# Six of seven expert searches on packed free tokens, low bits of each threshold from eight candidates, and eleven staging places for the gates' weights

## The chip, the core and the metric

The kernel runs on one core of a Trainium2 chip. The metric is device time in microseconds (us) of one execution. The engines are named as in the profile: PE (TensorE), DVE (VectorE), ACT (ScalarE), POOL (GpSimd) and SP (SyncE, which here issues DMAs). PEld is the weight load of TensorE.

## The reference

Three layers follow one another over 20224 tokens (4 sequences of 5056) of width 256. The first is a gated recurrence along each sequence. The other two are mixtures of 8 experts, each a two-layer network 256 to 1024 to 256.

```python
for t in range(S):                       # 1: recurrence
    h = f[:, t] * h + i[:, t] * x[:, t]
cap = N // E                             # 2: greedy assignment, 2528 tokens per expert
for idx in np.argsort(-logits.flatten()):
    tok, e = idx // E, idx % E
    if assigned[tok] >= 0 or counts[e] >= cap:
        continue
    assigned[tok] = e; counts[e] += 1
out[assigned == e] = np.maximum(x[mask] @ w1[e], 0) @ w2[e]
gate_w = softmax(x @ w_gate).max(-1)     # 3: best expert of each token, weighted
out[expert_idx == e] = gate_w * (np.maximum(x[mask] @ w1[e], 0) @ w2[e])
```

The greedy assignment is what the change is about. It falls into eight phases: in each, every free token wants its best expert among those not full; the next expert to fill has a threshold logit, all wishes above it are granted, and that expert leaves. Phases 0 to 6 need a search for the threshold; phase 7 gives the rest to the last expert.

## The kernel before, in words

**Stages.** A first stage reads the inputs in 40 pieces and runs the recurrence (`block`, lines 259 to 333). Then the first mixture (`moe1`) runs 16 lists: lists 0 to 7 hold, for each expert, 1024 tokens that a quick partial search already knows (`quick`, table `idxa`); lists 8 to 15 hold, in the order in which the experts fill, the other tokens (`compact_b`, table `idxb`). A list is made of blocks of 256 tokens: 4 blocks in each of lists 0 to 7, 6 in each of lists 8 to 15, 80 in all. A block fetches its rows by two indirect DMAs on POOL (L1218), turns them on PE (L1165), multiplies by the first weights (`up`, L1188) and the second (`down`, L1206), each product split in three float32r matmuls (high, low, cross), so a block has 48 matmuls of L1188 and 48 of L1206. `hand` scatters the result by four indirect DMAs per two blocks (L1298). The second mixture (`slot2`) runs 83 more blocks.

**What sets the order.** PE, DVE, ACT and POOL run in an order written out beforehand: `Plan.add` takes each operation with an assumed cost, its dependences and a priority, and `emit` fixes one order for each engine. A small number is a high priority: `up`'s outputs have -1, block work 1 or 2, splits of weights and the gates 3, a search 5 (`BG`), and compaction 6 (`CB`). An indirect DMA is planned at 1.05 us of POOL. On the chip each engine keeps that order and waits where an operand is late. SP issues its DMAs in order as well.

**The search, `assign(ph)`.** The best logits of the free tokens stand in a table of 1280 columns (`lay8`, phases 0 to 3) or 640 (`lay4`, phases 4 to 6, after `relay`). Eight rounds fix the high 16 bits of the threshold, two bits a round: `count` compares the table with three values, one on DVE (L710) and two on ACT (L715), `sums` adds on PE (L721, L724), and DVE decides (L743). Eight more rounds fix the low 16 bits in the same way (L783). `update` removes what was granted, over all 160 columns and 8 experts. In phase 0 the first six rounds have the highest priority, and `quick` follows them.

**The gates.** `gates` multiplies all second weights of the first mixture by the gate weights of the second, in two halves of eight chunks. Each chunk (512 KB, L1025) is loaded to one of four staging places (two halves of `rb`, two of `sh`), transposed on PE (L1032, 8 of them), copied by ACT (L1036, 2) and multiplied (L1037, 4). The first `down` of the first block needs the first half, its later ones the second half.

**Weights.** `load_w(e)` reads the weights of expert e (L1059, L1060) into `r1` and `r2`, splits them into high and low parts (L1063 on ACT; L1065 on POOL for expert 0, L1067 on DVE) and stores the parts for later (L1083); `load_again` reads them back for lists 8 to 15 (L1105), after SP has read the expert's number `ei` (L1091).

## Time and profile before

| | us |
|---|---|
| median of three runs | 2357.04 (2356.72 to 2360.22) |
| the profiled execution | 2358.22 |
| its span, first to last instruction | 2356.4 |
| PE busy in the span | 2190.8 (93%) |
| DVE busy | 1412.1 (60%) |
| ACT busy | 1022.0 (43%) |
| POOL busy | 601.2 (26%) |

The page gives each engine's busy time and its share in 40 slices. A window of the trace gives the busy time of each engine in one stretch and the number of its instructions; with one source line it counts that line's instructions alone, so blocks can be counted: 48 matmuls of L1188 are one block. The waits name the engine and the line that ended an idle time. Matmuls are pipelined, so PE can be shown as busy while its instructions start further apart than at best.

### The profile page before, as it was taken

How to read it: one execution, taken by the hardware profiler on the slowest of the kernel's cores; microseconds unless marked ns; L12 is line 12 of the kernel's file. 1: busy time of each engine (PE TensorE's matmuls, PEld its weight loads, DVE VectorE, ACT ScalarE, POOL GpSimd, SP SyncE). 2: the span in 40 equal slices, each digit the busy share in tenths (PEclk: the TensorE clock that was granted, in tenths of full speed). 3: DMA queues.
4: the chain of work that ended last, by engine and by line, in shares of the span. 5: the costliest groups of instructions: out<-in, count | busy, mean ns of one | idle time of the engine just before them, and what ended most of it. 6: DMA issues, size and time to landing. Idle time of an engine off the chain costs nothing.

```text
span 2356.4 us, 48919 instructions
## 1 busy us (share of the span) xinstructions
PE 2190.8 (93%) x18005; PEld 2115.6 (90%) x18005; DVE 1412.1 (60%) x3985; ACT 1022.0 (43%) x2094; POOL 601.2 (26%) x721
## 2 busy tenths in 40 slices
PE   7886899999999999995868899999999999999998
PEld 6774579999999999995758899999999999999998
DVE  7898778787887786876664444344433443344432
ACT  4555656746746635464532222223322232223322
POOL 5333313333432332141214112111111111111111
PEclk9998999999999999997879999999999999999999
DMA  9889635544567543544223318411425232311240
GB/s 323 268 272 329 226 135 179 206 158 145 203 222 233 193 170 123 198 146 158 74 101 125 106 33 287 120 46 46 119 53 173 57 114 53 118 47 46 49 122 26
DMA packets 262713, 341.84 MB, mean 145 GB/s; under 512 B 128220, under 2 KB 220254, under 8 KB 250688
## 3 DMA queue, kind: packets, MB, share of 16 engines
q1 hardware_dynamic: 235824, 264.10, 35.4%
q0 software_dynamic: 26640, 74.52, 9.2%
q8 instruction: 144, 2.36, 0.4%
q14 instruction: 105, 0.86, 0.1%
HBM read 495.90 MB, written 133.35 MB: 267 GB/s over the span
## 4 chain that ended last, share of the span: by engine, by line
PE 37%; issue 35%; DVE 9%; POOL 5%; DMA 4%; ACT 2%; SPq 1%; POOLq 0%; DVEq 0%; ACTq 0%
PE yp L1206 17%; PE bank L1188 16%; POOL out_dram L1541 5%; PE bank L1165 1%; DVE hl L1193 1%; DMA rb<-in_moe_w_dram 1%; DMA xg<-x1d,idxb 1%; DMA xg<-xs 1%; DMA w2l<-wsp 1%; PE bank L1037 1%; ACT ohb L715 1%; DVE jkc L997 1%; DMA xs<-xr,di 0%; PE bank L1032 0%; PE pb L308 0%
## 5 line engine op out<-in xcount | busy, mean ns | idle before, releaser
L1193 DVE SCALAR_TENSOR_TENSOR hl<-bank,hh 128x512 fp32r<-128x512 f32 x652 | 449.5, 689 | 729.8 <-ACT hh L1192 728.8
L1192 ACT ACTIVATE hh<-bank 128x512 fp32r<-128x512 f32 x652 | 389.0, 597 | 870.1 <-PE bank L1188 863.3
L1206 PE MATMUL yp<-w2h,hh 128*128 128x264 f32 (+1 forms) x2176 | 622.4, 286 | 6.9 <-ACT xr L1256 3.0
L1188 PE MATMUL bank<-xh,w1h 128*128 128x256 f32 x2176 | 616.9, 284 | 9.6 <-DVE hl L1193 9.6
L1188 PE MATMUL bank<-xl,w1h 128*128 128x256 f32 x2176 | 619.7, 285 | 0.9 <-DVE xl L1175 0.9
L1206 PE MATMUL yp<-w2l,hh 128*128 128x264 f32 (+1 forms) x2176 | 619.7, 285 | 0.0
L1206 PE MATMUL yp<-w2h,hl 128*128 128x264 f32 (+1 forms) x2176 | 618.9, 284 | 0.0
L1188 PE MATMUL bank<-xh,w1l 128*128 128x256 f32 x2176 | 615.0, 283 | 0.0
L1188 PEld LDWEIGHTS bank<-xh,w1h 128*128 128x128 f32 x2176 | 413.5, 190 | 9.8 <-DVE hl L1193 9.8
L1206 PEld LDWEIGHTS yp<-w2h,hh 128*128 128x128 f32 x2176 | 412.2, 189 | 8.5 <-ACT xr L1256 3.2
L1188 PEld LDWEIGHTS bank<-xl,w1h 128*128 128x128 f32 x2176 | 414.1, 190 | 1.3 <-DVE xl L1175 1.3
L1188 PEld LDWEIGHTS bank<-xh,w1l 128*128 128x128 f32 x2176 | 414.5, 190 | 0.0
L1206 PEld LDWEIGHTS yp<-w2l,hh 128*128 128x128 f32 x2176 | 412.0, 189 | 0.0
L1206 PEld LDWEIGHTS yp<-w2h,hl 128*128 128x128 f32 x2176 | 411.0, 189 | 0.0
L1541 POOL DMA_INDIRECT out_dram<-xr,ii x166 | 163.5, 985 | 761.3 <-ACT xr L1535 714.6
L1298 POOL DMA_INDIRECT xs<-xr,di x160 | 168.0, 1050 | 403.0 <-issue 173.3
L1188 PE MATMUL bank<-xh,third 128*128 128x256 f32 x864 | 168.2, 280 | 2.5 <-ACT xh L1174 2.5
L1206 PE MATMUL yp<-third,hh 128*128 128x256 f32 x864 | 156.6, 279 | 0.0
L1218 POOL DMA_INDIRECT xg<-x1d,idxb x96 | 96.2, 1002 | 231.1 <-PE bank L1165 140.1
L1188 PEld LDWEIGHTS bank<-xh,third 128*128 128x128 f32 x864 | 140.2, 190 | 2.7 <-ACT xh L1174 2.7
L715 ACT ACTIVATE ohb<-U,lw 128x1280 f16<-128x1280 uint16 (+1 forms) x104 | 115.6, 1112 | 44.0 <-DVE lw L786 37.5
L1206 PEld LDWEIGHTS yp<-third,hh 128*128 128x128 f32 x864 | 132.1, 189 | 0.0
(399 smaller groups left out, 3059.1 us busy)
## 6 DMA issues: line engine op xcount, KB each, us to landing
third<-wsp SPq DMA_DIRECT2D x108, 1024.0 KB
w1h<-wsp SPq DMA_DIRECT2D x53, 1024.0 KB
w1l<-wsp SPq DMA_DIRECT2D x53, 1024.0 KB
w2h<-wsp SPq DMA_DIRECT2D x53, 1024.0 KB
w2l<-wsp SPq DMA_DIRECT2D x53, 1024.0 KB
xg<-xs SPq DMA_DIRECT2D x332, 64.0 KB
fl<-in_f_logit_dram SPq DMA_DIRECT2D x36, 512.0 KB
xl<-in_x_dram SPq DMA_DIRECT2D x36, 512.0 KB
```

What stands on the lines that cost most here:

```text
L715: lambda k=k: act.activation(jk2[:, :TN], src[:, :TN], AF.Sign, bias=t3[:, k:k + 1], scale=sc, accum_out=ca3[:, k:k + 1]),
L997: dve(0.3, lambda a=a, a0=a0, px=px: v.scalar_tensor_tensor(jk[a % 2], px()[:, a, 0:J], q1[:, a0 + a:a0 + a + 1], arow, op0=OP.is_equal, o ...
L1037: P.add("PE", GC[1], lambda e=e, h=h, gt=gt, acc=acc: pe.matmul(acc.tile[:E * E], wgz[:, h, (7 - e) * E:(15 - e) * E], gt, start=e == 0 an ...
L1165: pe.transpose(bk.tile[:, o:o + 128], x2[i4][:, k, h * 128:(h + 1) * 128], identf)
L1188: P.add("PE", 0.1192, lambda c=c, h=h, k=k, w_=w_, xx=xx, s_=s_: pe.matmul(bk.tile[:, c * G:(c + 1) * G], wt(q, w_)[:, h, s_], xx[i4][:, h ...
L1192: P.add("ACT", 0.48, lambda: act.activation(hh[hb], bk.tile, AF.Relu), [bk], [("hh", hb)], prio=-1)
L1193: P.add("DVE", 0.6, lambda: v.scalar_tensor_tensor(hl[hb], bk.tile, 0.0, hh[hb].bitcast(F32), op0=OP.max, op1=OP.subtract), [bk, ("hh", hb ...
L1206: P.add("PE", 0.1192 if wid == D else 0.1215, lambda i=i, s_=s_, k=k, x_=x_, w_=w_, fc=fc: pe.matmul(yp[:ms[i], i, 0:wid], x_[hb][:, s_], ...
L1218: P.add("POOL", 1.05, lambda i=i, j=j: pool.indirect_dma_start(out=x2[i4][:, i, :D], out_offset=None, in_=x1d, in_offset=bass.IndirectOffs ...
L1298: st = pool.indirect_dma_start(out=xs, out_offset=bass.IndirectOffsetOnAxis(ap=di[i2][:, i:i + 1], axis=0), in_=y[:, i, 0:D + 2], in_offse ...
L1541: st = pool.indirect_dma_start(out=out, out_offset=bass.IndirectOffsetOnAxis(ap=ii[i4][:, i:i + 1], axis=0), in_=ot[:, i, :D], in_offset=N ...
```

## The change

Phase 0 still searches all 1280 columns. In every search the eight low rounds are replaced by `among`: DVE takes the eight largest low halves of each of the 128 rows (`v.max`), one matmul spreads them within the expert's 16 rows, eight compares count, and the right candidate is picked. If a row would need more than eight, `over` is set.

After phase 0 `pack` writes the numbers of the free tokens of each partition (six `v.max`, five `match_replace`) into 48 columns, of which 46 can be filled, and fetches their eight logits each by 46 indirect DMAs on POOL from a copy of the logits in DRAM (`lgd`, written by `keep`). Searches 1 to 6 and `update` then work on 48 columns (a table of 384 instead of 1280 or 640); `lay4` and `relay` go. Compaction works on 158 + 46 = 204 columns instead of 158, two picks at a time instead of three, with one more ACT copy for each pair. A validity mask is applied to all blocks of lists 8 to 15 instead of the last ones. If a partition has more than 46 free tokens or `over` is set, the new `again()` repeats all of the first mixture (in place of `leftover`).

The gates' chunks get eleven staging places instead of four: `rb`, `sh`, `sl`, one of `xg`, and `r1` and `r2` in halves, so that the weights of expert 0 are loaded after the chunks in `r1` and `r2` have been read. The load of expert 1 and the store of expert 0 wait for the first block (`("did", 0)`).

```diff
-    def assign(ph):
-        lay = lay8 if ph < HALF else lay4
-        ns, TN = lay.ns, lay.cols
...
+    def assign(ph, full=False):
+        near = ph == 0 and not full
+        W = JT if ph == 0 or full else JW
+        nblk = W // 16
+        TN = nblk * 128
...
-        for i in range(8):
+        if not full:
+            among(TN, half, dve, mm, late_)
+        for i in range(8 if full else 0):
             th = lw3 if i else lw0
             count(U, "U", th, "lw3" if i else "lw0", -1.0, jd, i + 8)
...
+    def among(TN, half, dve, mm, late_):
+        bk, b2 = Bank(1), Bank(1)
+        dve(TN * 0.00104 + 0.1, lambda: v.max(mx8, U[:, :TN]), ["U"], ["mx8"])
+        dve(0.2, lambda: v.tensor_tensor(xp, mx8[:, :, None].to_broadcast([128, 8, 16]), nth[:, None, :].to_broadcast([128, 8, 16]),
+                                         op=OP.mult), ["mx8"], ["eqb"], late_())
+        mm(lambda: pe.matmul(bk.tile[:, :128], grpf, xp.rearrange("p i r -> p (i r)"), start=True, stop=True), ["eqb"], [bk], n=2.5)
...
+        for i in range(8):
+            dve(0.28, lambda i=i: v.tensor_scalar(Thj[:, :128], bk.tile[:, :128], mx8[:, i:i + 1], None, op0=OP.is_ge, op1=OP.add,
+                                                  accum_out=n8[:, i:i + 1]), [bk, "mx8"], ["n8", "Th"])
...
+        dve(0.07, lambda: v.scalar_tensor_tensor(over, mx8[:, 7:8], lof, over, op0=OP.is_ge, op1=OP.max), ["mx8", "lof"], ["over"])
...
+    def keep():
+        P.add("POOL", 2.2, lambda: pool.tensor_copy(Lr, L.rearrange("p e j -> p j e")), ["L", "C"], ["C"], prio=1)
+        P.add("SP", 0.5, lambda: sp.dma_start(lgd.rearrange("(p j) e -> p j e", j=JT), Lr), ["C"], ["lgd"], prio=3, lat=5.0)
...
+    def pack():
+        for i in range(JW // 8):
+            t8 = k48[:, 8 * i:8 * i + 8]
+            dve(0.25, lambda t8=t8: v.max(t8, val), ["val"], ["k48"])
+            if i < JW // 8 - 1:
+                dve(0.25, lambda t8=t8: v.match_replace(val, t8, val, 0.0), ["k48"], ["val"])
...
+        for j in range(J2):
+            P.add("POOL", 1.05, lambda j=j: pool.indirect_dma_start(
+                out=G2[:, j], out_offset=None, in_=lgd, in_offset=bass.IndirectOffsetOnAxis(ap=gix[:, j:j + 1], axis=0)),
+                  ["gix", "L", "lgd"], [("G2", j)], prio=BG, lat=2.5)
+        dve(0.5, lambda: v.tensor_tensor(L2[:, :, :J2], G2.rearrange("p j e -> p e j"), vn[:, None, :J2].to_broadcast([128, E, J2]),
+                                         op=OP.min), [("G2", j) for j in range(J2)] + ["vn"], ["L"])
...
-        parts = [(t[:, k * 4 * D:(k + 1) * 4 * D], (f"g{y}", k), (y if y == "rb" else ("sh", k))) for y, t in (("rb", rb), ("sh", shf)) for k in range(2)]
+        parts = [(rb[:, k * 4 * D:(k + 1) * 4 * D], [("grb", k)]) for k in range(2)]
+        parts += [(t[k].bitcast(F32), [(key, k)]) for t, key in ((sh_, "sh"), (sl_, "sl")) for k in range(2)]
+        parts += [(xg[1].rearrange("p k c -> p (k c)")[:, :4 * D], [("xg", 1, k) for k in range(4)])]
+        parts += [(t.rearrange("p a b -> p (a b)")[:, k * 4 * D:(k + 1) * 4 * D], [(key, k)]) for t, key in ((r1, "r1"), (r2, "r2"))
+                  for k in range(2)]
...
-        P.add("SP", 0.5, lambda: sp.dma_start(r1, w1v[:, e]), [], ["r1"], prio=1, lat=5.0)
+        go = [("did", 0)] if e == 1 else []
+        P.add("SP", 0.5, lambda: sp.dma_start(r1, w1v[:, e]), go, [("r1", 0), ("r1", 1)], prio=1, lat=5.0)
...
     assign(0)
-    verdict()
+    keep()
+    pack()
     compact_b(0)
     for ph in range(1, E):
-        if ph == HALF:
-            relay()
```

## Rows read from the trace of the kernel before

**Rows 1.** Windows: stretch, length, busy PE PEld DVE ACT POOL, clock, DMA, GB/s
```profile
340.00:700.00 360.00, 355.80 (x3015) 350.87 (x3014) 299.23 (x988) 227.41 (x408) 122.74 (x117) 1.00 0.53 181
700.00:1085.00 385.00, 377.40 (x3189) 371.62 (x3188) 290.43 (x1019) 222.48 (x418) 112.14 (x111) 1.00 0.51 172
1085.00:1250.00 165.00, 101.22 (x780) 92.93 (x778) 105.74 (x445) 64.70 (x142) 40.44 (x42) 0.76 0.37 140
```
**Rows 2.** Windows of line L1188 alone: stretch, length, busy PE and PEld (counts)
```profile
340.00:700.00 360.00, 190.03 (x1365) 172.87 (x1366) 1.00 0.53 181
400.00:500.00 100.00, 54.19 (x391) 49.17 (x389) 1.00 0.50 172
700.00:1085.00 385.00, 200.67 (x1446) 182.78 (x1445) 1.00 0.51 172
1085.00:1300.00 215.00, 73.22 (x516) 66.84 (x517) 0.82 0.32 119
```
**Rows 3.** Waits of PE, 1040 to 1260: us in total, times, longest
```profile
PE msc L989 <- DVE jkc L997: 12.2, 6, 4.5
PE bank L1165 <- DMA xg<-x1d,idxb: 6.2, 6, 3.6
```
**Rows 4.** DVE in order of time: tables of lists 13 and 14
```profile
1125.02 0.17 DVE L973 TENSOR_TENSOR idxb<-jv,q 128x6 int32<-128x6 f32 x1
...
1239.37 0.17 DVE L973 TENSOR_TENSOR idxb<-jv,q 128x6 int32<-128x6 f32 x1
```
**Rows 5.** Line L802, ends of searches: count, ns min/median/max, first and last start
```profile
L802 DVE TENSOR_REDUCE es<-w x7: 150/152/161, 330.8 to 1223.2; 128x1 f32<-128x8 f32 x4, 128x1 f32<-128x4 f32 x3
```
**Rows 6.** Line L743, rounds of searches 1 (1280 columns) and 5 (640 columns)
```profile
L743 DVE SCALAR_TENSOR_TENSOR ge<-msc,remh,pws x7: 210/212/221, 386.7 to 429.5; 128x3 f32<-128x3 f32 x7
...
L743 DVE SCALAR_TENSOR_TENSOR ge<-msc,remh,pws x7: 215/220/222, 1012.7 to 1050.6; 128x3 f32<-128x3 f32 x7
```
**Rows 7.** Groups of DVE, 340 to 1260; one MAX8 in order of time
```profile
L710 DVE TENSOR_SCALAR_CACHE_REDUCE Th<-U,lw 128x1280 f16<-128x1280 uint16 x24 | 37.1, 1544 | 0.4
L997 DVE SCALAR_TENSOR_TENSOR jkc<-msc,q,arow 128x158 f16<-128x158 f32 x96 | 34.3, 378 | 4.8 <-ACT pv L994 3.9 <-PE msc L724 0.6
...
243.54 0.33 DVE L844 MAX8 m<-val 128x8 f32<-128x158 f32 x1
```
**Rows 8.** Indirect DMAs on POOL: in order, all of idxb, landing (340 to 700)
```profile
250.67 0.96 POOL L1218 DMA_INDIRECT xg<-x1d,idxa  x1 [0.30 <-issue]
251.93 0.95 POOL L1218 DMA_INDIRECT xg<-x1d,idxa  x1 [0.30 <-issue]
...
L1218 POOL DMA_INDIRECT xg<-x1d,idxb x96: 950/957/1975, 612.8 to 1293.2; - x96
...
DMA to landing us min/median/max: 2.7/2.9/7.8
```
**Rows 9.** Windows of all engines around the start of the first mixture
```profile
209.00:260.00 51.00, 25.49 (x112) 14.81 (x113) 37.71 (x114) 31.49 (x59) 22.69 (x20) 0.70 0.96 335
260.00:311.00 51.00, 46.33 (x253) 26.86 (x252) 35.22 (x113) 34.51 (x68) 7.76 (x8) 0.99 0.41 124
```
**Rows 10.** Windows of line L1032, then of line L1037 alone, the second stretch
```profile
260.00:311.00 51.00, 10.85 (x76) 8.12 (x76) 0.99 0.41 124
...
260.00:311.00 51.00, 22.73 (x46) 5.14 (x46) 0.99 0.41 124
```
**Rows 11.** Waits of SP, 209 to 311: us in total, times, longest
```profile
SPq L1025 <- PE bank L1032: 49.0, 11, 12.6
```
**Rows 12.** Groups of ACT, 209 to 311
```profile
L1036 ACT ACTIVATE xr<-bank 128x512 f32<-128x512 f32 x32 | 17.8, 590 | 2.1 <-PE bank L1032 2.1
```
**Rows 13.** SP in order of time: expert 0's weights, first chunk, expert 1's
```profile
211.75 0.37 SPq L1059 DMA_DIRECT2D r<-in_moe_w_dram  x1
...
212.68 2.25 SPq L1025 DMA_DIRECT2D rb<-in_moe_w_dram  x2
...
226.92 0.39 SPq L1059 DMA_DIRECT2D r<-in_moe_w_dram  x1
```

More of the change, by code (lines that the diff above doesn't have):

```diff
@@ L213 @@
     NTW = 3 * NSL
-    HALF = E // 2
     FLAG = 1 << 15
@@ L223 @@
     wsp = dram.tile([128, E, 4, H * F], F32, name="wsp")
+    lgd = dram.tile([128 * JT, E], F32, name="lgd")
     w1sp = dram.tile([128, E, 2, H * F], F32, name="w1sp")
@@ L661, in mm @@
             P.add("PE", 0.11 * n, fn, r, w, prio=1 if c else 0)
-        for g in range(turned if near else 0, lay.nb, 3):
-            n = min(3, lay.nb - g)
+        for g in range(turned if near else 0, nblk, 3):
+            n = min(3, nblk - g)
             bk = Bank(1)
@@ new lines, in dve @@
+        def dve(cost, fn, r, w):
+            P.add("DVE", cost, fn, r, w, prio=BG)
+        amp, n = (amap, J) if full else (amap2, JW)
+        dve(0.07, lambda: v.tensor_reduce(e1, es[:, :E - 1], axis=AX.X, op=OP.add), [("es", i) for i in range(E - 1)], [("es", E - 1)])
+        dve(0.07, lambda: v.tensor_scalar(e1, e1, -1.0, float(E * (E + 1)), op0=OP.mult, op1=OP.add), [], [("es", E - 1)])
+        sure(e1, E - 1, dve)
+        dve(0.14, lambda: v.tensor_scalar(cs[:, :n], amp, 0.0, e1, op0=OP.is_equal, op1=OP.mult), ["amap", ("es", E - 1)], ["cs"])
@@ L1583, in leftover @@
         table()
-        for s in range((E * (CAP - NB * 128) + E * (G - 1)) // G):
+        for s in range(2 - NE, NT2):
             slot2(s)
```

463 lines of the change are left out of this document (260 added, 203 removed).

## The prediction

> **What bounds the kernel now.** I read four views in this order: the windows of all engines, the windows of one line, the waits of PE, and the chain around the start of the first mixture. The windows say that PE is the bound nearly everywhere: it is busy for 355.8 of 360 us from 340 to 700 and for 377.4 of 385 us from 700 to 1085 [rows 1]. From 1085 to 1250 it is busy for 101.2 of 165 us only, and its mean granted clock falls to 0.76 of full speed, so part of the stretch runs at 1.2 instead of 2.4 GHz [rows 1]. A second hole, at the start of the first mixture, comes below with the gates.
>
> Counting L1188, with 48 to a block, turns this into blocks [rows 2]. From 400 to 500 the 391 matmuls are 8.15 blocks, or 12.28 us each. From 340 to 700 the 1365 are 28.4 blocks, or 12.66 us. From 700 to 1085 the 1446 are 30.1 blocks, or 12.78 us. From 1085 to 1300 the 516 are 10.75 blocks in 215 us, or 20 us each. As the rate of an undisturbed block beside light searches I take 12.47 us, the midpoint of 12.28 and 12.66.
>
> The waits of the slow stretch say who is late: PE stands behind the pick of the compaction (L989 on jkc) and behind rows fetched by idxb [rows 3]. The table of list 13 is written at 1125.0 [rows 4], 40 us into the hole, and that of list 14 at 1239.4, 114 us later, where six blocks need 75. So the searches are late, not the mixture. The seven ends of a search lie between 330.8 and 1223.2 [rows 5]: 148.7 us for one.
>
> **Searches 1 to 6.** A round takes (429.5 - 386.7)/6 = 7.1 us at 1280 columns and (1050.6 - 1012.7)/6 = 6.3 us at 640 [rows 6]. Halving the table saves only 0.8 us, since a round mostly waits for its low-priority turn on DVE, ACT and PE. At 384 columns I take 6.0 us (ends 5.5 and 6.3). Eight rounds go and eight become shorter: 16 x 7.1 - 8 x 6.0 = 66 us less. `among` comes in their place: one pass over the table, which is below the 1.54 us that a pass over 1280 columns takes [rows 7], about twenty small DVE operations and two trips to PE. That is two rounds' worth, 14 us (ends 8 and 25). The shorter `update` I leave uncounted. A search then takes about 148.7 - 66 + 14 = 97 us.
>
> Search 0 loses eight rounds as well and gains one `among`: its end moves from 330.8 to about 330.8 - 8 x 7.1 + 14 = 288. `pack` is new in front of search 1. Its eleven MAX8-like operations at 0.33 us [rows 7] and some twenty small ones are 8 us of DVE, at a priority at which 2 us of work take a 7 us round, so 30 us. Its 46 gathers take 0.96 + 0.30 us each [rows 8], 58 us of POOL. POOL is otherwise busy for 122.7 of 360 us, with 0.30 us ahead of each of 117 instructions [rows 1], 44%, so 58 us need about 104. Then `pack` ends near 288 + 30 + 104 = 422, search 5 near 422 + 5 x 97 = 907 and search 6 near 1004. A compaction adds some 25 us. List 13 begins where the hole begins, at 1085; with the 35 us that the steps below save ahead of it, it will want its table near 1050, and list 14 six blocks later, near 1125. **So the late searches stop costing anything**, with about 100 us to spare. What is next late there is PE's own work: 215 - 10.75 x 12.47 = 81 us saved (79 to 83 by the two rates).
>
> The stretch from 340 to 1085 also gains: 58.6 blocks took 745 us and at 12.47 take 730, 15 us less (0 if the rate stays at 12.72, 26 at 12.28), since fewer rounds put small matmuls between the block's and fewer 1.5 us passes stand ahead of hl on DVE.
>
> **Costs put at nothing.** The picks grow from 158 to 204 columns (96 of 0.38 us, [rows 7], some 10 us of DVE in all), each pair of picks adds an ACT copy, and each second block of lists 8 to 15 a mask operation. DVE and ACT idle for 61 and 133 of the 360 us of the first stretch [rows 1] and the searches that filled them shrink. Without that cover they would cost 25 us. The copy that `keep` makes on POOL (planned at 2.2 us) and its store fall into the start, where POOL is busy for 22.7 of 51 us [rows 9]; no cover would make that 5 us. Expert 1's load now waits on SP for the first block, with the stores of expert 0, and nothing behind it in that queue is due sooner. Three blocks, 37 us, remain for 2 MB (6 us at the 335 GB/s of [rows 9]) and sixteen splits of about 0.6 us on ACT and DVE; if they are late, list 1 waits for some us, which is in the range.
>
> **The gates.** The 64 multiplications and 128 transposes sit on PE's path, and 22.7 + 10.9 = 33.6 us of them fall after 260 [rows 10], when blocks could run. SP waited 49 us in eleven waits for a staging place to be read [rows 11]: staging is what holds the chunks back. With eleven places they can run while PE idles for 25.5 us from 209 to 260 [rows 9]. ACT must copy 32 tiles at 0.59 us [rows 12] beside the quick rounds, where it is busy for 31.5 of 51 us, and expert 1's splits leave this stretch. The first chunk no longer stands behind the 2 MB of expert 0 [rows 13]. I take six chunks moved ahead at 33.6/10 us: 20 us (ends 0 and 33.6). Against it: `r1` and `r2` are now free for expert 0 only after chunks 7 to 10 have been read. Eleven chunks from 213 on are 17 us of loads and, at 3.4 us each on PE, end near 255, so its weights come about when the first block can start anyway. The DMA queues were 96% busy from 209 to 260 [rows 9]; expert 1's 2 MB [rows 13] and the stores of expert 0 leave, and seven earlier chunks and the 0.65 MB of `lgd` enter, which is about even.
>
> **A new stall.** The written order plans an indirect DMA at 1.05 us of POOL; it takes 1.26. For `pack` the planner fills all of POOL's gaps, so over 46 gathers and, in eight blocks, some 33 fetches and scatters between them POOL falls 79 x 0.21 = 17 us behind. PE's turns of the fetched rows and DVE's one operation behind all gathers stand at planned places and wait, and the block's work waits behind them. PE and DVE fall behind the plan somewhat themselves, which the trace doesn't size; I take 12 us lost, once (ends 0 and 56, below), near the full lag.
>
> **The sum.** 81 + 15 + 20 - 12 = 104 us off the profiled execution's 2358.2 (span 2356.4 and 1.8 around it), which is 2254; that execution is 1.2 us above the median of the runs, so 2253.
>
> **Rivals.** (a) Staging gives nothing, because expert 0's weights come late by what the earlier gates save: 2253 + 20 = 2273. For it: r1 and r2 are read last. Against it: PE has 25 us idle to fill.
>
> (b) The gathers are held up. The longest fetch took 1.98 us against a median of 0.96 [rows 8]. At that length each is 1.98 + 0.30 - 1.05 = 1.23 us over plan, and 46 cost 56 us instead of 12: 2297. Against it: the median, with DVE busy for 83% of 340 to 700 [rows 1]. The Trainium skill (SBUF — State Buffer, Who interferes with whom) has a rule that speaks for it: a VectorE instruction with two inputs in SBUF and a GpSimd instruction that reads SBUF exclude each other for a whole instruction. By that rule the time would go towards that of (b); the trace bears it out for a few fetches at most.
>
> (c) The searches stay late, half as much as now: 2253 + 40 = 2293. It needs searches of 120 us or more.
>
> (d) **Slower than before**: each gather waits until the one before it has landed, as all write one tile. A fetch lands 2.9 us after its issue [rows 8]; with issue and gap a gather would hold POOL for up to 4.2 us, and 46 x (4.2 - 1.05) = 145 us of fetches behind them would be late: 2253 - 12 + 145 = 2386. It turns the sign from 1.05 + (104 + 12)/46 = 3.6 us a gather. Against it: two fetches into one tile start 1.26 us apart [rows 8].
>
> (e) The change doesn't do what it says: a partition with over 46 free tokens sets off `again()`, and 80 blocks at 12.47 us, near 1000 us, come on top. From the reference's inputs, 2656 tokens are free after phase 0, at most 32 in a partition, so this is remote.
>
> (f) All goes well: 83 + 26 + 33 = 142 us, 2216.
>
> **How the numbers follow.** Chances: forecast 0.55, (a) 0.14, (b) 0.10, (c) 0.06, (d) 0.06, (e) 0.01, (f) 0.08. From 2215 to 2297 the range takes in all but (d) and (e), and the ends of the unknown costs. A measurement tells 0.2% (4.7 us) from no change. Faster by more has 0.92, within it 0.01, slower 0.07.
>
> **What would show it.** Right: PE's windows between 1000 and 1250 show no hole and a full clock; the last search ends near 1000 and its table is written 75 us or more before PE asks; over 20 of the 32 gate copies come before the first up; the first block starts before 260 and its second weights before 275. A hole of some 10 us near 350 to 430 with PE or DVE behind a gather would show the new stall. Wrong: a hole that moved to weights or SP, rounds no shorter than 7 us and more of them waiting, a first block after 265, or an execution that grows by a repeated mixture.

## The result, and the profile after

| | before | after |
|---|---|---|
| median (lowest to highest), us | 2358.18 (2356.72 to 2360.22) | 2321.78 (2316.31 to 2325.02) |
| the profiled execution, us | 2358.22 | 2325.02 |
| its span, us | 2356.4 | 2323.2 |

The ratio is 0.9843 with a 95% interval of 0.9819 to 0.9866: 36 us faster, where 104 were forecast (2253, range 2215 to 2297). The sign and the main term were right, the sum was not. The profiled execution of after is the slowest of its four.

First the page of after (busy us and share of each engine, then tenths busy in 40 slices, and the granted clock in tenths), then windows of all engines, which answer [rows 1].

```profile
PE 2193.2 (94%) x17886; PEld 2125.4 (91%) x17886; DVE 1297.3 (56%) x3899; ACT 857.0 (37%) x1922; POOL 639.2 (28%) x766
PE   7887786999999999999999899999999999999997
PEclk9998998999999999999999999999999999999998
```
```profile
340.00:700.00 360.00, 333.08 (x2763) 326.26 (x2762) 275.92 (x1183) 169.96 (x409) 126.70 (x127) 0.97 0.49 171
700.00:1085.00 385.00, 378.63 (x3181) 373.78 (x3180) 249.57 (x994) 158.37 (x344) 122.52 (x123) 1.00 0.58 197
1085.00:1250.00 165.00, 165.00 (x1387) 164.84 (x1387) 74.50 (x221) 52.62 (x93) 55.90 (x56) 1.00 0.42 148
```

The hole from 1085 to 1250 is gone: PE is busy for all of 165 us, at a clock of 1.00, where [rows 1] had 101.2 us and 0.76. But from 340 to 700 PE is now idle for 27 us, where it was idle for 4.

To see where the rest went I count main matmuls, those of the first and second weights. 96 of them are the work of one block, and the place of block n is the start of the 96n-th. PE runs ups of the next block between downs of the running one, so a place tells how far the work has come and not when that block itself is done (the 48th down starts at 110.7 before and 110.3 after). The table gives the places in us after the last scan of the first stage (L293 of before; it starts at 205.4 before and 212.8 after). Four kernels of the last two groups, below, stand beside them.

| block | before | after | e11 | e14 | e15 | e16 |
|---|---|---|---|---|---|---|
| 1 | 80.0 | 92.1 | 82.8 | 82.3 | 80.4 | 83.8 |
| 3 | 134.5 | 135.3 | 120.6 | 120.2 | 127.4 | 123.8 |
| 4 | 146.9 | 165.6 | 132.5 | 132.1 | 139.3 | 135.7 |
| 8 | 199.4 | 219.1 | 183.3 | 183.0 | 189.0 | 201.8 |
| 50 | 732.5 | 770.7 | 748.0 | 750.9 | 747.4 | 753.7 |
| 62 | 885.4 | 915.2 | 894.5 | 897.4 | 897.1 | 897.6 |
| 74 | 1115.5 | 1059.6 | 1038.4 | 1041.3 | 1041.0 | 1041.5 |
| 80 | 1197.6 | 1142.5 | 1121.2 | 1124.3 | 1124.3 | 1124.5 |
| 160 | 2105.8 | 2060.3 | 2029.2 | 2032.4 | 2032.6 | 2032.7 |

Differences of its columns, with the first stage and the end, make up the 33.2 us by which the two spans differ:

| stretch | gained, us | forecast |
|---|---|---|
| first stage, to the last scan | -7.4 | 0 |
| to block 3 (gates, first weights) | -0.8 | 20 |
| block 3 to 4 (12.4, then 30.3) | -17.9 | -12 |
| block 4 to 62 | -11.1 | 15 |
| block 62 to 74 (230.1, then 144.4) | 85.7 | 81 |
| block 74 to 160 | -10.4 | 0 |
| after block 160 (45.2, then 50.1) | -4.9 | 0 |

**The searches.** Ends of searches (L823, answering [rows 5]), tables (L1047), rounds of searches 1 to 6 (L759): count, ns min/median/max, first and last start.

```profile
L823 DVE TENSOR_REDUCE es<-w x7: 153/155/158, 286.6 to 856.7; 128x1 f32<-128x8 f32 x7
...
L1047 DVE TENSOR_TENSOR idxb<-jv,q x16: 154/166/167, 311.3 to 906.7; 128x6 int32<-128x6 f32 x16
...
L759 DVE SCALAR_TENSOR_TENSOR ge<-msc,remh,pws x42: 208/216/222, 397.8 to 838.0; 128x3 f32<-128x3 f32 x42
```

Search 0 ends at 286.6, search 6 at 856.7, 366 us sooner than in [rows 5], and the last table is written at 906.7.

**The new hole.** Waits of PE, 250 to 450, and of DVE, 300 to 400 (us in total, times, longest), then the 46 gathers on POOL and DVE in order of time:

```profile
PE yp L1286 <- DVE hl L1273: 17.2, 1, 17.2
PE msc L648 <- DVE eqb L647: 3.8, 1, 3.8
PE msc L1026 <- DVE rr L1023: 3.0, 1, 3.0
...
DVE L L961 <- DMA L<-lgd,gix: 21.5, 1, 21.5
...
L958 POOL DMA_INDIRECT L<-lgd,gix x46: 940/944/1416, 303.0 to 371.4; - x46
...
373.59 0.81 DVE L961 TENSOR_TENSOR L<-L,vn 128x368 f32<-128x368 f32 x1 [21.54 <-DMA L<-lgd,gix]
374.44 0.56 DVE L976 TENSOR_TENSOR L<-L,p 128x384 f32<-128x384 f32 x1
374.92 0.68 DVE L1146 TENSOR_TENSOR w1l<-r,w1h 128x512 fp32r<-128x512 f32 x1
375.52 0.68 DVE L1273 SCALAR_TENSOR_TENSOR hl<-bank,hh 128x512 fp32r<-128x512 f32 x1
```

DVE stands for 21.5 us at the one operation that needs all gathers. The hl of the running block is the third behind it, and PE waits 17.2 us for that hl.

**The gates.** Waits of SP from 209 to 311 (answering [rows 11]), the loads of expert 0's weights on SP, and the windows of [rows 9]:

```profile
SPq L1138 <- PE bank L1110: 18.0, 1, 18.0
SPq L1139 <- PE bank L1110: 11.5, 1, 11.5
...
260.87 0.37 SPq L1138 DMA_DIRECT2D r<-in_moe_w_dram  x1
285.37 0.37 SPq L1139 DMA_DIRECT2D r<-in_moe_w_dram  x1
...
209.00:260.00 51.00, 35.41 (x166) 19.67 (x165) 42.52 (x155) 31.79 (x67) 14.96 (x18) 0.84 0.75 245
260.00:311.00 51.00, 40.53 (x213) 27.58 (x213) 43.71 (x159) 20.03 (x46) 24.55 (x23) 0.90 0.54 168
```

PE does 9.9 us more before 260 than in [rows 9]. But the load of `r1` is issued at 260.9 and that of `r2` at 285.4, and the first up starts at 267.0 (258.9 before), the first down at 292.6 (279.7 before). Counted from the last scan that is 54.2 us (53.5) and 79.8 us (74.3). From 260 to 311 PE is busy for 5.8 us less than in [rows 9].

### The profile page after: what moved, and what is told of

Its sections match the earlier page's. It is cut to its first block, busy times and chain, and to the rows that moved or that the text cites. A ratio compares the mean times of both kernels' runs of the same rounds, so it can differ in the third digit from the quotient of the medians.

```text
span 2323.2 us, 48550 instructions
## 1 busy us (share of the span) xinstructions
PE 2193.2 (94%) x17886; PEld 2125.4 (91%) x17886; DVE 1297.3 (56%) x3899; ACT 857.0 (37%) x1922; POOL 639.2 (28%) x766
## 5 line engine op out<-in xcount | busy, mean ns | idle before, releaser
L1286 PE MATMUL yp<-w2h,hl 128*128 128x264 f32 (+1 forms) x2176 | 620.9, 285 | 17.2 <-DVE hl L1273 17.2
L1268 PE MATMUL bank<-xh,w1h 128*128 128x256 f32 x2176 | 618.1, 284 | 10.1 <-DVE hl L1273 10.1
L1286 PE MATMUL yp<-w2h,hh 128*128 128x264 f32 (+1 forms) x2176 | 621.7, 286 | 4.0 <-DVE lg L1333 1.8
L1268 PE MATMUL bank<-xl,w1h 128*128 128x256 f32 x2176 | 621.9, 286 | 0.0
L1286 PE MATMUL yp<-w2l,hh 128*128 128x264 f32 (+1 forms) x2176 | 620.1, 285 | 0.9 <-DVE w2l L1146 0.9
L1268 PE MATMUL bank<-xh,w1l 128*128 128x256 f32 x2176 | 616.5, 283 | 1.8 <-POOL w1l L1144 1.8
L1286 PEld LDWEIGHTS yp<-w2h,hl 128*128 128x128 f32 x2176 | 412.2, 189 | 17.5 <-DVE hl L1273 17.4
L1268 PEld LDWEIGHTS bank<-xh,w1h 128*128 128x128 f32 x2176 | 414.4, 190 | 10.5 <-DVE hl L1273 10.3
L1286 PEld LDWEIGHTS yp<-w2h,hh 128*128 128x128 f32 x2176 | 412.8, 190 | 6.0 <-DVE lg L1333 2.2
L1268 PEld LDWEIGHTS bank<-xh,w1l 128*128 128x128 f32 x2176 | 415.3, 191 | 2.6 <-POOL w1l L1144 2.0
L1268 PEld LDWEIGHTS bank<-xl,w1h 128*128 128x128 f32 x2176 | 415.0, 191 | 0.0
L1286 PEld LDWEIGHTS yp<-w2l,hh 128*128 128x128 f32 x2176 | 412.7, 190 | 1.4 <-issue 1.1
L1371 POOL DMA_INDIRECT xs<-xr,di x160 | 161.4, 1009 | 190.3 <-issue 111.8
L1298 POOL DMA_INDIRECT xg<-x1d,idxb x96 | 98.3, 1024 | 349.2 <-PE bank L1245 183.0
L1268 PE MATMUL bank<-xh,third 128*128 128x256 f32 x864 | 171.8, 282 | 2.3 <-ACT xh L1254 2.3
L1286 PE MATMUL yp<-third,hh 128*128 128x256 f32 x864 | 159.2, 282 | 0.0
L1268 PEld LDWEIGHTS bank<-xh,third 128*128 128x128 f32 x864 | 141.1, 190 | 2.6 <-ACT xh L1254 2.6
L1286 PEld LDWEIGHTS yp<-third,hh 128*128 128x128 f32 x864 | 132.9, 189 | 0.2 <-ACT xr L1615 0.2
L1268 PE MATMUL bank<-xl,third 128*128 128x256 f32 x432 | 122.0, 282 | 0.3 <-DVE xl L1255 0.3
```

The lines of the kernel that those rows point to most:

```text
L1268: P.add("PE", 0.1192, lambda c=c, h=h, k=k, w_=w_, xx=xx, s_=s_: pe.matmul(bk.tile[:, c * G:(c + 1) * G], wt(q, w_)[:, h, s_], xx[i4][:, h ...
L1286: P.add("PE", 0.1192 if wid == D else 0.1215, lambda i=i, s_=s_, k=k, x_=x_, w_=w_, fc=fc: pe.matmul(yp[:ms[i], i, 0:wid], x_[hb][:, s_], ...
L1298: P.add("POOL", 1.05, lambda i=i, j=j: pool.indirect_dma_start(out=x2[i4][:, i, :D], out_offset=None, in_=x1d, in_offset=bass.IndirectOffs ...
L1371: st = pool.indirect_dma_start(out=xs, out_offset=bass.IndirectOffsetOnAxis(ap=di[i2][:, i:i + 1], axis=0), in_=y[:, i, 0:D + 2], in_offse ...
```

## The experiments

The kernels come in five groups. Those of one group share a chip and the runs of the kernel before. In the first three groups that kernel took 2388 to 2395 us, in the last two 2358 to 2360, as above, so times are compared within a group, and ratios across groups. Each ratio has its 95% interval. Every kernel here computes everything.

### First group: which part of the start costs

**c0_before** is the kernel before again.

> The kernel before once more, profiled, as a yardstick for what differs between two profiled executions of one program. In the first profile of before the last scan of the first stage starts at 205.4 us and a matmul of the second mixture (1800 to 2270 us) follows the one before it after 117.2 ns (up) and 117.8 ns (down); in the profile of after it is 212.8 us, 118.5 and 118.9 ns, with the same instructions. If these differences belong to the execution or the chip, this run moves by as much (205 to 213 us, 117 to 119 ns). If they belong to the change, it repeats 205.4 within 1 us and 117.5 within 0.3 ns.

2390.45 us, blocks 1 and 4 at 82.6 and 148.4 after the scan. The chip takes longer, but not the matmuls: their step, below, is that of the first profile (117.17 and 117.80 ns).

**e1_seven**: the gates' chunks no longer pass through `r1` and `r2`.

```diff
-        parts += [(t.rearrange("p a b -> p (a b)")[:, k * 4 * D:(k + 1) * 4 * D], [(key, k)]) for t, key in ((r1, "r1"), (r2, "r2"))
-                  for k in range(2)]
```

> After, with the gates' chunks staged in seven places: r1 and r2 are left to expert 0 alone. Theory (late weights): in after the second weights are loaded at 285.4 us, because the last chunk in r2 is transposed only at 284.7; without it both loads of expert 0 leave before 235, the first block ends 73 to 78 us after the start of the search (85 in after), and the execution gets 7 to 14 us shorter, 2308 to 2315 by the median of 2321.8. Rival (PE and ACT are full with the gates, the place of staging doesn't matter): the first block ends no earlier than 83 us after the search's start, since fewer chunks are ahead of it, and the time is 2320 or more.

2391.78 us, ratio 0.9985 (0.9972 to 0.9999). Block 1 is at 82.4, 7 us sooner than in after on such a chip (89.5, c1_after): the late weights do hold block 1. But block 4 is at 186.9 (c1_after 181.9), so nothing of it is left there. In the total seven places gain nothing over eleven (c1_after has 0.9972); whether they are worse the two intervals don't tell.

**e2_gather126** plans a gather at what it takes.

```diff
-            P.add("POOL", 1.05, lambda j=j: pool.indirect_dma_start(
+            P.add("POOL", 1.26, lambda j=j: pool.indirect_dma_start(
```

> After, with each of pack's 46 gathers planned at 1.26 us of POOL instead of 1.05, which is what it takes with the gap ahead of it; nothing else. Theory (the plan is too short): DVE's operation behind all gathers, where DVE waits 21.5 us and PE behind it 17.2 us (359 to 376 us) with the clock falling to 1.2 GHz, is written some 10 us later and PE's hole shrinks below 6 us; 10 to 16 us less in all, 2306 to 2312. Search 1 starts later by about 10 us, which costs nothing. Rival (the gathers crowd the fetches out of POOL, whatever the plan says): the hole stays at 12 us or more, now behind a fetched row, and the time is 2317 or more.

2382.72 us, 0.9961 (0.9947 to 0.9976). It couldn't tell: on this chip PE has no hole behind the gathers to remove.

**e6_old_staging** has the four old staging places and the old start of expert 1's weights.

```diff
-        parts = [(rb[:, k * 4 * D:(k + 1) * 4 * D], [("grb", k)]) for k in range(2)]
...
+        parts = [(t[:, k * 4 * D:(k + 1) * 4 * D], [(y, k)]) for y, t in (("grb", rb), ("sh", shf)) for k in range(2)]
...
-        go = [("did", 0)] if e == 1 else []
+        go = []
...
```

> After, with the whole part on the gates undone: four places (rb, sh) as before, expert 1's load and expert 0's stores without their new place. By the prediction's term the new staging is worth 20 us, so this would take 2342. By the theory of late weights the new staging gains about as much in PE work moved ahead as its late second weights give back, so this takes 2312 to 2325, with the first block ending 71 to 77 us after the start of the search and the gates' remaining work after it. In both cases the hole behind pack's gathers stays.

2398.22 us, 1.0016 (1.0005 to 1.0028); after has 0.9972 on such chips. By these ratios, of two groups, the staging is worth 0.44%, some 10 us there, where 20 were forecast.

### Second group: the tail, and the top-8

**c1_after** is the changed kernel again.

> The changed kernel again, on the chip on which e1, e2 and e6 ran beside a before of 2395 us instead of 2358. Theory (chip): there the whole middle of any kernel runs slower, and this run takes some 2377 to 2390 us, a ratio of 0.992 to 0.998, with blocks 50 to 74 in about 305 us as in e1, e2 and e6 instead of 288.8. Rival (the order): the ratio repeats 0.984 (2355 to 2360 us if before is 2395) and blocks 50 to 74 take 288 to 290 us, so that the three edits each lost some 25 us by the new order that any edit of the plan brings. The last scan of the first stage starts at 208 to 213 us in either case if it belongs to the changed program.

2381.06 us, 0.9972 (0.9962 to 0.9983): here the change gives 7 us, not 36. In the trace of c1_after ACT starts 34 of the 652 hidden tiles 0.7 to 3.8 us after both the up that they wait for and its own work have ended, 58 us in all (19 and 34 us in c0_before); in the two first traces there is none. And of the 29 us that are missing against after, most go between blocks 1 and 2: 47.7 us in c1_after, 27.7 in after, but 38.9 in c0_before and 40.1 in before. All kernels with the change take 44 to 54 us there in the first three groups, 24 to 35 in the last two. Windows of all engines in c1_after:

```profile
310.00:320.00 10.00, 5.00 (x8) 0.85 (x6) 0.95 (x5) 0.91 (x3) 7.56 (x9) 0.67 0.06 3
320.00:330.00 10.00, 0.77 (x3) 0.13 (x2) 0.94 (x5) 0.68 (x3) 4.66 (x5) 0.50 0.05 2
```

PE, DVE and ACT nearly stand for 20 us while POOL issues gathers; DVE starts one small operation of the compaction (L1066) at 328.2, 13.7 us after the matmul that it reads has ended. Instructions and their order are the same as in after. Why engines start late on these chips stays open.

**e7_pad** adds two unused tiles, so that the mixtures' tiles lie at the addresses of before. After's differ by 256 bytes for most of them and by 480 for the weights of the even experts, so the distances between the two changed by 224.

```diff
+    pad0 = cst([128, 64], F32, "pad0")
...
+    pad1 = rt([128, 56], F32, "pad1")
```

> After with two unused tiles, 256 bytes ahead of the large tiles and 224 bytes ahead of a part of them, which put the weights, the split rows and the hidden tiles of the mixtures at the addresses that they have in before; the order of the instructions is that of after but for two small memsets. In before an up matmul of the second mixture follows the last after 117.2 ns and a down after 117.8; in after, e1, e2 and e6 alike 118.5 and 118.9. Theory (the place of the operands): back to 117.2 and 117.8, blocks 80 to 160 in 908 to 910 us instead of 918, 9 us from there and some 4 more from the first mixture: 0.5 to 0.6% under the run of after on the same chip. Rival (something else of the changed program): 118.5 and 118.9 stay, and the time is that of after within 0.2%.

2372.35 us, 0.9925 (0.9907 to 0.9943): 8.7 us below c1_after, 0.47% by the ratios. The mean distance from one matmul's start to the next in the second mixture is 117.16 ns for L1268 and 117.78 for L1286, as before (117.17 and 117.78); in after it is 118.52 and 118.87. The same count by windows of 1450 to 2250 (all engines; the number in brackets behind PE's busy time counts its matmuls), in before, in after and in e16, which has the pad too:

```profile
1450.00:2250.00 800.00, 797.50 (x6774) 797.31 (x6775) 321.84 (x568) 238.33 (x426) 139.57 (x142) 1.00 0.31 84
...
1450.00:2250.00 800.00, 800.00 (x6739) 799.84 (x6738) 316.55 (x561) 235.44 (x421) 137.69 (x140) 1.00 0.29 78
...
1450.00:2250.00 800.00, 800.00 (x6814) 800.00 (x6814) 320.97 (x568) 238.21 (x426) 139.13 (x143) 1.00 0.29 79
```

With PE busy for all of 800 us and a clock of 1.00, after gets through 6739 matmuls and e16 through 6814, 1.1% more.

**e4_low8** puts the eight low rounds back into searches 1 to 6, on the packed tokens.

```diff
+        low8 = full or ph > 0
-        if not full:
+        if not low8:
...
```

> After, with the eight rounds on the low bits back in searches one to six, on the packed table of 384 columns; search 0 keeps the top-8 way. This tells what the rounds alone are worth. By the prediction's steps a round at 384 columns is 6.0 us and the top-8 way 14, so each of the six searches grows by 34 us to some 115 (from 81 in after), the last ends at 860 + 6 x 34 = 1060, and its lists' tables at about 1100: blocks 62 to 74 lose at most 10 us, but blocks 8 to 62 gain a little as the same small matmuls are spread further. Total within 10 us of after on the same chip. Rival (the low rounds were what made the searches late): the last tables come after 1150, PE stands still for 40 us or more between 1050 and 1250, and the time is 40 us or more over after.

2382.15 us, 0.9970 (0.9958 to 0.9981), the time of c1_after. Packing, with the shorter search 0, is enough to cure the late searches; that `among` shortens searches 1 to 6 further moves nothing. `among` without packing was not tried.

**e5_j32** packs into 32 columns, with 32 gathers.

```diff
-    J2, JW = 46, 48
+    J2, JW = 32, 32
...
```

> After, with room for 32 free tokens in a partition instead of 46 (table of 256 columns instead of 384, 32 gathers instead of 46, picks of 224 columns instead of 252). The most that a partition holds is 32. Theory: POOL's lag behind the plan falls from 60 x 0.21 = 12.6 to 46 x 0.21 = 9.7 us and the gathers end 17 us earlier, so the hole behind them (17.2 us in after) is 12 to 14; a pick costs PE 0.01 us less, a pass over the table 0.13 us less: 5 to 10 us under after on the same chip. Rival (the hole is the sum of the gathers' own time and not of the plan's error): it shrinks by 14 x 1.25 = 17 us to nothing, and 15 us or more are gained.

2361.07 us, 0.9884 (0.9866 to 0.9902), 20 us below c1_after. By e7, some 9 to 11 of them are the matmuls' step again: its sizes happen to give 117.16 and 117.78 ns.

### Third group: which distance, and all together

**c2_after**

> The changed kernel once more, as the yardstick of this call. On the first chip (before 2357 to 2360 us) it took 0.984 of before, and PE stood 17.2 us behind DVE's operation after the gathers; on the second (before 2387 to 2401 us) 0.997, PE was 30 us late by then and the hole measured under 1 us, while ACT began 27 of some 270 hidden tiles 0.7 to 2.4 us after their up group had ended (none on the first chip; in before 13, 18 us together, on the second and none on the first). If those late starts belong to the chip, this run shows none of them beside a before of about 2358, and 25 to 30 beside one of about 2390.

2381.6 us, 0.9978 (0.9968 to 0.9987).

**e8_pad32** has `pad1` with 8 columns only, so that all tiles stand alike within 64 bytes, as before, at distances changed by 192.

> After with one unused tile of 32 bytes, which moves the weights of the even experts and of the second mixture's third set by 32 bytes, back to the same place in a 64-byte line as the rows that they meet. Theory (the 64-byte phase): the up step of even lists falls from 118.3 to 116.0 ns as in before, e7 and e5, that of odd lists stays at 119.5, the second mixture's steps are 117.2 and 117.8, and the time is 0.4 to 0.6% under after of this call. Rival (another distance counts, which e7 restored and this doesn't): 118.3 stays, and the time is that of after.

2384.02 us, 0.9984 (0.9974 to 0.9994); steps 118.84 and 118.39. The place within 64 bytes is not what counts.

**e9_pad32_g126** is e8 with the gathers planned at 1.26.

> e8 with pack's gathers planned at 1.26 us instead of 1.05. Theory (plan too short): where the run of after in this call shows a hole of 17 us behind DVE's operation after the gathers, this shows under 6 and is 8 to 16 us faster than e8; where after shows no such hole, it is within 5 us of e8. Rival (the gathers' own time): the hole stays above 12 us.

2376.16 us, 0.9943 (0.9923 to 0.9962), 8 us below e8 though there was no hole behind the gathers to remove. The new cost also changes the written order from block 4 on; that this is the reason is not shown, and in e2 the same edit is not told apart from c1_after.

**e10_all** joins 32 columns, gathers at 1.26 and `keep`'s copy on ACT.

```diff
...
-        P.add("POOL", 2.2, lambda: pool.tensor_copy(Lr, L.rearrange("p e j -> p j e")), ["L", "C"], ["C"], prio=1)
+        P.add("ACT", 1.4, lambda: act.activation(Lr, L.rearrange("p e j -> p j e"), AF.Copy), ["L", "C"], ["C"], prio=1)
```

> After with room for 32 free tokens in a partition (which also puts weights and rows at one 64-byte phase), gathers planned at 1.26 us, and the copy of the table on ACT instead of POOL. Theory for the copy: POOL's copy of 2.35 us (220.4 to 222.7) runs beside DVE's copy of 128 columns, which takes 2.16 us instead of some 0.2; on ACT, DVE's takes 0.2 to 0.4 and the first round starts 1 us earlier at least. Rival: DVE's copy is slow by itself and stays at 2 us. In all: 1.0 to 1.6% under after of this call, the sum of the phase (0.5%), the smaller room (0.4%) and up to 0.6% for the hole where there is one.

2354.06 us, 0.9863 (0.9846 to 0.9879). What `keep` costs is seen in three lines: POOL's copy in after, DVE's copy beside it, and the same DVE copy in e10.

```profile
220.37 2.35 POOL L906 COPY C<-L 128x1280 f32<-128x1280 f32 x1 [7.58 <-PE msc L685]
...
220.64 2.16 DVE L691 COPY Th<-T 128x128 uint16<-128x128 uint16 x1 [0.94 <-ACT T L689]
...
215.50 0.23 DVE L691 COPY Th<-T 128x128 uint16<-128x128 uint16 x1 [0.94 <-ACT T L689]
```

DVE's copy is held for as long as POOL's lasts. But on ACT the copy takes 2.38 us ahead of ACT's own first count, and the first round comes no sooner.

### Fourth group: is pack in the way of the first blocks?

**e11_late** has `pad1` of e7 and plans everything behind search 0 80 us later; **e13_packlate** does so for pack and what follows it alone; **e12_all_late** is e10 with the 80 us. The edit in e11 and e12:

```diff
...
-        dve(0.14, lambda: v.tensor_tensor(amp[:, :Jc], amp[:, :Jc], cs[:, :Jc], op=OP.add), ["amap", "cs"], ["amap"])
+        dve(0.14, lambda: v.tensor_tensor(amp[:, :Jc], amp[:, :Jc], cs[:, :Jc], op=OP.add), ["amap", "cs"], ["amap"], 80.0 if near else 0.0)
```

> After, with everything that hangs on search 0's last operation (the compaction of list 8, pack, the searches behind it) planned 80 us later, so that it no longer falls into the first four blocks; and an unused tile of 224 bytes that puts weights and rows at the distance that they have in before (both 256 bytes lower). Theory (collision): between the first stage's last scan and block 4 the kernel of before takes 147 to 148 us, after 166 on the first chip and 182 on the second; without pack and compaction there it takes 150 to 160, the last tables come near 990, still ahead of their lists, and the time is 15 to 25 us under after of the last call, the phase of the operands (10 us) included. Rival (the work costs what it costs wherever it lies): block 4 gains, but blocks 4 to 16 lose as much, and only the 10 us of the operands' place are gained. The distance: if it is what counts, the up step of even lists is 116.0 ns and the second mixture's steps 117.2 and 117.8, as in e7; else 118 to 119.

> After with the same 224 bytes and pack alone (its 46 gathers and all searches behind it) planned 80 us later; the compaction of list 8 stays where it is, in the first block. Theory (the gathers are what the start pays for): block 4 as early as in e11 within 5 us. Rival (the compaction and the gates are what it pays for): block 4 as late as in after, 178 to 184 us behind the last scan on the second chip, and e11 is 15 us or more faster.

> e10 (room for 32, gathers at 1.26, copy on ACT) with everything behind search 0 planned 80 us later. By the theory of the collision another 10 to 20 us under e10, that is a ratio to before of 0.978 to 0.982; by the rival the same as e10, 0.986.

2293.42 us, 0.9730 (0.9714 to 0.9746); 2299.19, 0.9756 (0.9739 to 0.9773); and **2281.59, 0.9674 (0.9658 to 0.9689)**, the best version of all, 77 us below before. These ran on a chip like that of the first profiles; no kernel with the 80 us ran on a chip of the first three groups, so what e12 gains over e10 (0.9863) is not the 80 us alone. Blocks 1 to 4 run well (table). I took this for the collision shown. The traces made me doubt: the hole hadn't gone, it had moved with the gathers. Waits of DVE in e11 (430 to 470), e13 and e12 (400 to 470):

```profile
DVE L L963 <- DMA L<-lgd,gix: 15.6, 1, 15.6
...
DVE L L963 <- DMA L<-lgd,gix: 15.4, 1, 15.4
...
DVE L L960 <- DMA L<-lgd,gix: 7.3, 1, 7.3
```

### Fifth group: lag, collision and staging apart

**e14_late_g126** is e11 with the gathers planned at 1.26; **e15_late_old** is e14 with e6's staging; **e16_pad_g126** is e14 without the 80 us.

> e11 (place of before, all behind search 0 planned 80 us later) with pack's 46 gathers planned at 1.26 us. Theory of the lag: the wait of PE behind the gathers, 12.2 us in e11, falls below 4 us and the total by 8 to 12 us, to near 0.969 of the time before where that is 2358. Rival, the wait comes from something else that stands at that place: it stays within 2 us of 12.2 and the total within 3 us of e11.

> e14 with the four old staging places and the old start of expert 1's weights. This sizes the staging by itself, with the first blocks clear of pack. If the prediction's 20 us is right, 17 us or more over e14, nearly all of it before block 4. If r1 and r2 give most of the gain back, 0 to 8 us over e14.

> e14 without the 80 us: pack again beside the first blocks, with its gathers planned at 1.26 us and the places of before. Theory of the collision: block 1 ends 8 us or more later after the last scan than in e14, block 4 15 to 25 us later, and the total is 8 to 18 us over e14, as the wait behind the gathers is no part of it any more. Rival, all the loss was the lag: within 4 us of e14, and block 1 no later.

2294.10 us, 0.9733 (0.9712 to 0.9754); 2295.09, 0.9734 (0.9715 to 0.9754); 2299.24, 0.9758 (0.9735 to 0.9781). Three theories of mine were tried, and none came out as I put it. The written order holds a planned start for each operation, and against it a trace shows which engine is late.

The lag first: e14 is no faster than e11, and PE's longest wait is 14.0 us. Waits of DVE in e14 (420 to 470), e15 (460 to 500) and e16 (340 to 380); the first is put down to a fetch, but L963 needs the gathers:

```profile
DVE L L963 <- DMA xg<-x1d,idxa: 12.1, 1, 12.1
...
DVE L L963 <- DMA L<-lgd,gix: 7.6, 1, 7.6
...
DVE L L963 <- DMA L<-lgd,gix: 14.7, 1, 14.7
```

The gathers are not all that falls behind. POOL in e14, between two gathers:

```profile
373.49 0.94 POOL L960 DMA_INDIRECT L<-lgd,gix  x1 [0.30 <-issue]
376.81 1.02 POOL L1373 DMA_INDIRECT xs<-xr,di  x1 [2.38 <-issue]
378.14 1.45 POOL L1373 DMA_INDIRECT xs<-xr,di  x1 [0.30 <-issue]
379.89 0.98 POOL L1373 DMA_INDIRECT xs<-xr,di  x1 [0.30 <-issue]
381.18 1.28 POOL L1373 DMA_INDIRECT xs<-xr,di  x1 [0.30 <-issue]
382.77 0.99 POOL L1300 DMA_INDIRECT xg<-x1d,idxa  x1 [0.30 <-issue]
384.06 1.31 POOL L1300 DMA_INDIRECT xg<-x1d,idxa  x1 [0.31 <-issue]
385.68 1.24 POOL L960 DMA_INDIRECT L<-lgd,gix  x1 [0.30 <-issue]
```

Four scatters and two fetches keep the gathers off POOL from 374.4 to 385.7, 11.3 us, where the order has 6 times 1.05 or 6.3: a lag of 5 us in one place, with the gathers' own cost mended. From the first gather to the last, POOL falls 16.6 us behind the order in e11, 15.4 in e13, 11.3 in e14 and 7.5 in e15, while PE keeps to it; DVE waits 15.6, 15.4, 12.1 and 7.6 us. So there the hole is the lag of the whole queue, and with 32 gathers instead of 46 (and gathers at 1.26) it shrinks to 7.3 us (e12). In e16 it is not: POOL falls only 3.7 us behind (70.9 us where the order has 67.2) and DVE still waits 14.7, because PE has come 11.8 us ahead of the order from block 2 to block 3 (14.0 us, planned 25.8).

The collision: e16 has pack beside the first blocks and yet has block 1 only 1.5 us later than e14, block 4 3.6 us later, and takes 5 us longer, not 8 to 18. Its hole comes ahead of block 8 and that of e14 behind it; from block 62 on the two are level, and the 3.6 us between their spans lie ahead of the last scan (211.1 and 207.6). So of the 27 us between after and e11, by their ratios, 5 to 7 at most are the deferral, and behind the last scan the traces show none of it; 20 come without it.

Between the profiled executions of after and e16 it is 29 us, since e16's is its fastest. Of these the matmuls' step is 9.7 us from block 80 to 160 alone (917.9 and 908.2 in the table). 17.3 lie ahead of block 8 (219.1 and 201.8), and 11.5 of them ahead of block 3, where the planned cost of the gathers cannot be the reason: up to block 4 PE runs the same order in both. In after PE stands at two small matmuls of the searches among the first blocks' (L648 and L1026 in the waits above, 6.8 us); in e16 it waits at neither. DVE and POOL in after, and the same DVE operation in e16:

```profile
267.51 5.60 DVE L873 SCALAR_TENSOR_TENSOR nu<-val,thr,nu 128x158 f16<-128x158 f32 x1
267.94 4.98 POOL L1144 TENSOR_TENSOR w1l<-r,w1h 128x512 fp32r<-128x512 f32 x4
...
267.04 0.38 DVE L875 SCALAR_TENSOR_TENSOR nu<-val,thr,nu 128x158 f16<-128x158 f32 x1
```

A small operation of 0.4 us takes 5.60 in after: it ends when POOL is through with four splits of expert 0's first weights, and the decision of search 0 that L648 needs stands behind it on DVE. In e16 it is done before POOL's run gets going. e12 meets the same (5.61 us, and 3.9 us of PE at that matmul), so it is a matter of half a microsecond and not of the order. Beside the four splits of the second weights, 292.5 to 297.6, four more small operations of DVE take 1.2 to 1.4 us each in after, ahead of the wait at L1026.

The staging: e15, with the old places, is 7.2 us later at block 4 and 6.0 at block 8, but level at block 62, and the totals differ by 1 us. With the new staging DVE waits 12.1 us behind the gathers, with the old one 7.6, so 4.5 of the 6.0 us are gone at that wait. Why POOL lags more in e14 than in e15 is not isolated.

## Why the prediction was wrong in its size

**The late searches (81 us) were right**: 85.7 us from block 62 to 74, 12.03 us a block where I took 12.47. The steps to it erred on the careful side. (One reading was crooked: 1125.0 is the first half of list 13's table and 1239.4 the second half of list 14's. Like for like the two are 110 us apart, which changes nothing.) A round of search 1 takes 5.7 us (L759 at 397.81 and, six rounds on, at 431.84; 6.0 forecast), a search (856.7 - 449.4)/5 = 81.5 us (97), by its ends. Search 0 ended at 286.6 (288), pack at 374 (422), search 6 at 857 (1004). The reserve of 100 us became some 220 (list 14's table is done at 889.2, its first fetch starts at 1110.8), and e4 shows that nothing hung on it.

**The stretch from 340 to 1085 (15 us) had the wrong sign.** From block 4 to 62 the kernel lost 11.1 us: 18.5 from block 8 to 50 (533.1 us, then 551.6) and 1.0 ahead of it, less 8.4 that came back behind it. The step that failed is "fewer rounds put small matmuls between the block's". The rounds of searches 5 and 6 and the picks of the late lists used to stand behind block 50, most of them in the hole, where PE idled; now they stand here, between main matmuls. Windows of the picks alone, 400 to 1000, before (L989) and after (L1063):

```profile
400.00:1000.00 600.00, 4.57 (x36) 2.28 (x36) 1.00 0.55 187
...
400.00:1000.00 600.00, 16.31 (x84) 5.03 (x84) 1.00 0.52 179
```

84 picks instead of 36, each of 252 columns on PE instead of 160. By the distances between main matmuls from block 8 to 50 they cost 11.0 us instead of 2.6, rounds 6.6 instead of 4.2, `among` 3.7 and the turns of the table (L685) 0.8 more: 15.3 of the 18.5 us. I had covered the wider picks by idle DVE and ACT; their price was on PE, which had no cover.

**The staging (20 us) came to nothing.** Up to block 3 it lost 0.8 us. The gates' work did move: 84 of the 128 transposes come before the first up, 52 before the change. Of the 32 copies it is 18, where the prediction's sign asked for over 20, and 11 before the change. Windows of the copies alone from the last scan to the first up, before (L1036) and after (L1114):

```profile
205.40:258.87 53.47, 6.06 (x11) 0.71 0.96 331
...
212.70:267.00 54.30, 10.12 (x18) 0.87 0.73 239
```

What failed is "end near 255": the last chunk in `r2` was transposed at 284.7, and SP held the load of `r2` for it until 285.4. The gates' transposes have a lower priority than the ups, so the written order has this one 8.3 us behind the first up; in the trace it comes 17.7 behind it. PE waited 1.8 us for a part of the weights and 3.8 at L648, and after that wait, from 277 to 282.8, the granted clock was 0.50, the lower level, at which the ups follow each other after 0.21 us instead of 0.12. So from the last scan the first down started 5.5 us later than before (13 us by the trace's own time, 7.4 of them the first stage's). That is rival (a)'s mechanism, and the prediction's signs of being wrong show it: the first up came behind 265, and the second weights behind 275. Where the start is clear (e14, e15) the staging brings 7 us by block 4, and the wait behind the gathers takes most of them back.

**The new stall (12 us) was there, and larger**: block 4 came 17.9 us late, behind one wait of DVE of 21.5 us. Place and mechanism are as forecast; the term was mis-sized. The lag is smaller than I had it: 46 gathers and the 8 other indirect DMAs between the first and the last make 54 times 0.21, 11.3 us (I had 79 and 17 us); the first and the last gather start 68.4 us apart, and the written order has 55.6, a lag of 12.8. The step that failed is "PE and DVE fall behind the plan somewhat themselves". The written order has block 3 end 25.8 us behind block 2; in the trace it ends 15.5 us behind it (119.8 and 135.3). So PE came 10 us ahead of the order while POOL fell behind, and the wait is what lay between the two. e16 and the late kernels show either part by itself, above.

**Not in the sum**: the step of the matmuls (10.4 us from block 74 to 160), 7.4 us in the first stage and 4.9 behind block 160. The change adds small tiles, and what lies behind them in SBUF moves; I had no row for that. I also had no term for DVE's small operations being held beside POOL's splits: PE waits 6.8 us for them ahead of block 1 (L648 and L1026). What the 4.9 us behind block 160 are stays open. The first stage's loss isn't isolated: the last scan starts between 204 and 213 in kernels whose code differs there only in added tiles or planned costs.

Together: 104 + 4.7 (late searches) - 26.1 (stretch) - 20.8 (staging) - 5.9 (stall) - 10.4 - 7.4 - 4.9 = 33.2 us, the difference of the spans.

**The rivals.** (b) did not happen: the 46 gathers took 0.944 us at the median and 1.416 at most. The Trainium skill's rule (SBUF — State Buffer, Who interferes with whom), that VectorE and GpSimd exclude each other for a whole instruction on a port that they share, which a plain copy on VectorE can take as well, shows in another place: DVE's copy took 2.16 us beside POOL's 2.35 us copy, and 0.23 us without it. The trace agrees there. The longest hold of this kind is that of L873 above, 5.60 us, over four instructions of POOL in a row. (c), (d) and (e) did not happen either: the searches were early, gathers started 1.25 us apart, and no block was repeated. Nor did (f), in which all goes well.

## What to carry to other kernels

A hole that closes doesn't give all its length: the work that stood in it moves to where the bound engine is busy, and its instructions on that engine must be priced there. In a fixed order, time won ahead of a slow chain of another engine is waited for at the first operation that stands behind that chain, so a gain is priced at the last such operation, not where it arises. When a change adds tiles, compare the step of an untouched stretch before and after: if it moved, the places of the operands did it.

## What the hardware showed unasked

- The same matmuls, with the same shapes and a granted clock of 1.00, start 117.17 ns apart at one set of places of their operands in SBUF and 118.52 at another (L1188 and L1268; 117.78 and 118.87 for the second weights). A pad of 224 bytes brings the first back. Distances changed by 224 and 192 bytes are slow, by 768 (e5) as fast as before; equal places within 64 bytes aren't enough (e8). Which rule lies behind it stays open.
- The same program gains 1.6% on one chip and 0.2 to 0.3% on two others, where ACT starts some tiles 0.7 to 3.8 us after what they wait for and DVE one operation 13.7 us after. The cause stays open.
- A DVE operation of 0.4 us (two inputs in SBUF) took 5.60 us in after and 5.61 in e12 beside four POOL operations in a row that read SBUF (4.98 us); where it was done before they began it took 0.38 (e16).
